# A spectral layer and an MLP on one core: the transforms' steps moved to earlier ticks, and one more block by Strassen's scheme

## Chip, cores and metric

The kernel runs on one core of one Trainium2 chip. The metric is the device time of one execution in microseconds (us). Engines: TensorE (PE; its weight loads are shown as PEld), VectorE (DVE), ScalarE (ACT), GpSimd (POOL) and the queue that issues most DMAs (SP).

## What is computed

```python
# x: (4, 3008, 256); w_r, w_i: (256, 256); w_in: (256, 2048); w_out: (2048, 256)
X = np.fft.rfft(x, axis=1)
Yr = X.real @ w_r - X.imag @ w_i + b_r
Yi = X.real @ w_i + X.imag @ w_r + b_i
Y = shrink(Yr) + 1j * shrink(Yi)          # sign(v) * max(|v| - 0.01, 0)
y = np.fft.irfft(Y, n=3008, axis=1).reshape(12032, 256)
h = y @ w_in
out = (h / (1 + np.exp(-h))) @ w_out
```

All of it is float32; the kernel gets there with pairs of float32r numbers, a high and a low part, so that most products are three matmuls.

## The kernel before

**The MLP** sets the beat. The 12032 tokens are 24 blocks of up to 512, the 2048 hidden units 16 slices of 128. A block and a slice are one *tick*, 384 in all (`ticks`, L1059: slices 0 to 7 of block 0, all of block 1, the rest of block 0 from tick 24 on, then blocks 2 to 23, block i at ticks 16i to 16i+15). In a tick (L1190 to L1228) the recording order is: the shrink left over from the tick before (`deferred`), `split_g` of the tick before (gh on ACT, gl on DVE), `mlp1` (12 matmuls of 256 columns, then Silu on ACT), what the table `fill` has for tick t, `run` (`mlp2` with the slice of two ticks ago: 12 matmuls), and what `fill` has for t + 0.5. Every engine works through its own share of this in order. At a boundary tick, 16i+1, `mlp2` ends block i-1: ACT copies the first half of the accumulators to `o`, DVE the second (L816); in tick 33 DVE also adds the first half of block 0 to both (L819). The same stands at tick 25 for block 1, without the adds.

**Blocks in `FAST`** (10 to 22) do `mlp1` for two slices together by a Strassen scheme (`fast_one`, `fast_more`, `fast_two`, L739 to L785): 7 half products of 3 matmuls in place of 24 matmuls. `fast_moving` (L687, POOL and ACT) makes the sums of x for a block, `fast_weights` (L667) those of w_in, once, after `swap_pools` (L1161) has given up the transforms' pool.

**The transforms** of sequences 1 to 3 lie in the fills (sequence 0 is done before tick 0). Each has 12 units u of two frequencies. `u3_step(b, u, 0)` (L961) issues the DMAs for unit u+2, runs `s2_3(u)` (4 products, PE; casts on ACT and DVE), `split_z(u-2)` (zh on ACT, zl on DVE) and `i1(u-3)` (6 matmuls, then the copy `i1o` on ACT, L505). `u3_step(b, u, 1)` runs `mix3(u-1)` (L447): 6 matmuls into one PSUM bank, which ACT copies to q; then 12 into a second bank, which DVE reads in the shrink (y, L473 to L477). The shrink is deferred to the start of the next tick. Sequences 2 and 3 also need 16 *pieces* each, `stack_split` and `stack_product`. `i2(i)` and `i2_ends(i)` make the columns of block i.

**PSUM** has 8 banks: two of tag h, three acc, and one each of d0, d1 and e0. `bank` (L183) gives d0 and d1 by turns, `third_bank` (L194) gives e0. A matmul that is the first to write a newly given bank waits until the last reader of the bank's use before is done.

**The order of the fills** comes from the loop at L1112: from tick 24 on, each tick gets one stage (a piece, a step or a mix), and none at a boundary tick or one in `taken` (9, 25, and the 16i+1). By its rules the sequences end at ticks 72, 118 and 147.

## Time and profile before

| what | us |
|---|---|
| median of 3 runs (lowest, highest) | 1292.41 (1291.47, 1292.78) |
| the profiled execution: its time, its span | 1294.4, 1291.3 |
| PE busy in the span (10931 matmuls) | 1279.6 |
| DVE, ACT, POOL busy | 894.4, 790.3, 207.1 |

The span runs from the first to the last instruction; 3.1 us of the profiled execution lie around it, and that execution is 2.0 us over the median. Busy times say how much an engine did, not what it held up: who waited for whom is read from the list of waits and the timeline, and what ended last from the chain of waits. A row of the timeline gives start and duration, engine, line and operation; the bracket at its end, the time that the engine stood still before it and who released it. A row of waits gives total us, times and the longest. A row of a stretch gives its length, then busy us (and instructions) of PE, PEld, DVE, ACT and POOL, the granted TensorE clock (1.00 is 2.4 GHz), the DMA engines' share and GB/s.

### The profile page before, as it was taken

The numbers are of one execution on the slowest core, as the hardware profiler recorded it, in microseconds if no ns is written. First come the engines' busy times: TensorE is split into PE (matmuls) and PEld (weight loads), VectorE is DVE, ScalarE is ACT, GpSimd is POOL, SyncE is SP. The second block draws the span as 40 slices with busy tenths as digits, with TensorE's granted clock in tenths as the row PEclk, the third lists the DMA queues.
The fourth block names the chain that finished last, engine by engine and source line by source line (L and its number), as shares of the span: only waits on it lengthen the run. The fifth ranks groups of instructions, "written<-read, shape, count | busy, mean of one in ns | idle before, by whom it ended". The sixth has DMA issues, their size and how long they took to land.

```text
span 1291.3 us, 27533 instructions
## 1 busy us (share of the span) xinstructions
PE 1279.6 (99%) x10931; PEld 1255.5 (97%) x10931; DVE 894.4 (69%) x1703; ACT 790.3 (61%) x1640; POOL 207.1 (16%) x306
## 2 busy tenths in 40 slices
PE   7999999999999999999999999999999999999998
PEld 3989999999999999999999999999999999999998
DVE  4787757878768777666758766667666666676663
ACT  5556655767667657555555666666666666666655
POOL 3001002222212221112202110211012101110200
PEclk8999999999999999999999999999999999999999
DMA  7975514554465543424220111011101110110000
GB/s 263 288 229 191 142 52 122 133 152 109 117 168 148 128 132 99 135 77 122 82 71 2 48 33 29 5 33 33 27 12 34 32 33 1 33 33 14 4 24 25
DMA packets 76296, 110.30 MB, mean 85 GB/s; under 512 B 9008, under 2 KB 54952, under 8 KB 76168
## 3 DMA queue, kind: packets, MB, share of 16 engines
q1 hardware_dynamic: 61921, 79.17, 20.9%
q0 software_dynamic: 10672, 25.68, 7.9%
q10 hardware_dynamic: 3575, 3.70, 0.9%
q8 instruction: 86, 1.41, 0.4%
q14 instruction: 42, 0.34, 0.1%
HBM read 71.03 MB, written 37.49 MB: 84 GB/s over the span
## 4 chain that ended last, share of the span: by engine, by line
PE 97%; DMA 1%; DVE 0%; issue 0%; ACT 0%; POOL 0%; POOLq 0%
PE acc L804 40%; PE h L729 19%; PE h L643 17%; PE mix L454 6%; PE mix L394 3%; PE s L429 2%; PE i L501 2%; PE i2e L570 2%; PE i L570 2%; PE s L281 1%; PE s L320 1%; DMA x_pre<-in_x_dram 1%; PE s L363 1%; PE i L498 1%; PE i L563 1%; PE warm L918 1%
## 5 line engine op out<-in xcount | busy, mean ns | idle before, releaser
L804 PE MATMUL acc<-wout,gh 128*128 128x256 f32 x3008 | 539.8, 277 | 0.3 <-ACT gh L659 0.3
L804 PEld LDWEIGHTS acc<-wout,gh 128*128 128x128 f32 x3008 | 453.8, 188 | 1.5 <-issue 1.0
L804 PE MATMUL acc<-wout,gl 128*128 128x256 f32 x1504 | 415.8, 276 | 0.2 <-DVE gl L660 0.2
L804 PEld LDWEIGHTS acc<-wout,gl 128*128 128x128 f32 x1504 | 282.3, 188 | 0.4 <-DVE gl L660 0.4
L643 PE MATMUL h<-xt,win 128*128 128x256 f32 x2016 | 259.5, 277 | 0.4 <-ACT g L650 0.4
L643 PEld LDWEIGHTS h<-xt,win 128*128 128x128 f32 x2016 | 242.5, 188 | 1.1 <-ACT g L650 0.6
L650 ACT ACTIVATE g<-h 128x512 f32<-128x512 f32 (+1 forms) x177 | 101.9, 576 | 147.9 <-PE h L643 144.4
L780 DVE TENSOR_TENSOR gl<-gp,gh 128x512 fp32r<-128x512 f32 x208 | 145.9, 701 | 25.0 <-ACT gh L779 24.0
L767 ACT ACTIVATE gp<-gp 128x256 f32<-128x256 f32 x104 | 43.4, 417 | 180.1 <-DVE gp L764 180.1
L660 DVE TENSOR_TENSOR gl<-g,gh 128x512 fp32r<-128x512 f32 (+1 forms) x177 | 117.5, 664 | 46.8 <-ACT gh L659 45.1
L779 ACT CAST gh<-gp 128x512 fp32r<-128x512 f32 x208 | 129.3, 622 | 6.6
L659 ACT CAST gh<-g 128x512 fp32r<-128x512 f32 (+1 forms) x177 | 106.1, 600 | 1.1 <-PE acc L804 0.2
L729 PE MATMUL h<-xt,win 128*128 128x256 f32 x624 | 106.2, 279 | 0.0
L769 DVE TENSOR_TENSOR gp<-h,u 128x256 f32<-128x256 f32 x104 | 44.1, 424 | 78.7 <-ACT gp L768 78.7
L473 DVE TENSOR_TENSOR y<-q,mix 64x256 f32<-64x256 f32 x144 | 60.3, 419 | 41.2 <-PE mix L454 30.6
L729 PE MATMUL h<-th,sw_h 128*128 128x256 f32 x312 | 87.4, 280 | 0.0
L729 PEld LDWEIGHTS h<-xt,win 128*128 128x128 f32 x624 | 86.4, 188 | 0.1
L729 PE MATMUL h<-th,sw_l 128*128 128x256 f32 x312 | 86.2, 276 | 0.0
L729 PE MATMUL h<-tl,sw_h 128*128 128x256 f32 x312 | 86.2, 276 | 0.0
L461 POOL TENSOR_TENSOR q<-q,bias 128x256 f32<-128x256 f32 x36 | 29.9, 832 | 335.8 <-ACT q L460 335.8
L764 DVE TENSOR_TENSOR gp<-h,u 128x256 f32<-128x256 f32 x104 | 44.1, 424 | 50.2 <-PE h L729 48.6
L704 POOL TENSOR_TENSOR td<-xf 128x256 f32<-128x256 f32 x13 | 12.3, 948 | 339.0 <-ACT xf L604 260.9
(172 smaller groups left out, 2385.6 us busy)
## 6 DMA issues: line engine op xcount, KB each, us to landing
x_sb<-in_x_dram POOLq DMA_DIRECT2D x70, 188.0 KB, 4.0
a<-scr SPq DMA_DIRECT2D x48, 256.0 KB
gin<-scr SPq DMA_DIRECT2D x48, 192.0 KB
t<-in_c_dram POOLq DMA_DIRECT2D x36, 256.0 KB, 3.6
scr<-i1o SPq DMA_DIRECT2D x36, 256.0 KB
t<-in_c_dram SPq DMA_DIRECT2D x48, 128.0 KB
scr<-s1o SPq DMA_DIRECT2D x32, 192.0 KB
w<-in_moe_w_in_dram SPq DMA_DIRECT2D x8, 512.0 KB
```

What stands on the lines that cost most here:

```text
L454: nc.tensor.matmul(out=out, lhsT=x_[:, e, c, :], rhs=m[:, e, :], start=(n == 0), stop=(n == 5))
L473: nc.vector.tensor_tensor(out=y[64 * i:64 * i + 64, r, :], in0=q[rows, i, :], in1=pv[rows, i, :], op=op,)
L570: nc.tensor.matmul(out=p[:, o:o + NP + RR], lhsT=t[:, q:q + 128], rhs=c4_sb[:, h * (NP + RR):(h + 1) * (NP + RR)], start=(h == 0), stop=(h ...
L643: nc.tensor.matmul(out=p[:, c:c + D], lhsT=w[:, e, f * 128:(f + 1) * 128], rhs=v[:, e, c:c + D], start=(m == 0), stop=(m == 5),)
L650: nc.scalar.activation(out=g[:, q], in_=p[:, q], func=ACTF.Silu)
L659: nc.scalar.copy(gh[:, q], g[:, q])
L660: nc.vector.tensor_sub(gl[:, q], g[:, q], gh[:, q])
L729: nc.tensor.matmul(out=p, lhsT=w[j], rhs=m[k], start=(begins and n == 0), stop=(n == 2), skip_group_check=True,)
L764: nc.vector.tensor_tensor(out=g[:, 1, :], in0=px[:, 0:HB], in1=u, op=ALU.add)
L779: nc.scalar.copy(h, v)
L780: nc.vector.tensor_sub(l, v, h)
L804: nc.tensor.matmul(out=a[:, r, :], lhsT=v[:, q], rhs=wout[:, f, w, :], start=(begins and m == 0 and r == 0), stop=(ends and m == 2), skip_ ...
```

## The change

The loop is rewritten so that more stages fit in a tick. Steps may stand at boundary ticks and at tick 25, and the first is at tick 23 rather than 24. Units 12 to 14 of a sequence, which have no `s2_3`, share a tick with what follows: at ticks 61 and 130 the step of unit 12 and its mix, at tick 107 a step and a piece. In the last sequence the steps of units 5, 7, 9 and 11 take e0 and bring their mix along as a fill at t + 0.5, behind the units of `mlp2` (ticks 120, 123, 126 and 129). The sequences now end at ticks 65, 110 and 132. Before a sequence's first loads all pending stores are issued (`flush(16)`). Block 9 joins `FAST`: `mlp1` loses 192 matmuls of L643 and gains 168 of L729; no other matmul is added or taken away.

```diff
--- before.py
+++ after.py
@@ -34,7 +34,7 @@
 
 STACKED = 2
 
-FAST = range(10, 23)
+FAST = range(9, 23)
 
 X_BUFS = [0, 1, 2, 3, 4, 5, 6, 7, 6, 7, 3, 4, 0, 2, 1, 0]
 BLOCKS = [(c, min(BLK, NT - c)) for c in range(0, NT, BLK)]
@@ -1088,7 +1088,7 @@
         at(0, x_ahead)
         for i in range(2):
             put(5, s1_later, 7, i)
-        for t in (11, 35):
+        for t in (11, 34):
             at(t, x_ahead)
         at(30, nc.gpsimd.dma_start, c5_sb, c5)
         m3 = mix3_weights()
@@ -1108,15 +1108,45 @@
                           for k, fn in enumerate(((i2, i), (i2_ends, i))))
         stacked, last, begun = {1: 18}, 24, set()
         ended = {}
-        done, t, since = 37, 24, 0
+        done, t, since = 34, 23, 0
+        def put_piece(t, since):
+            nonlocal done
+            at(max(t - 2, done), stack_split, *pieces_left[0])
+            at(t, stack_product, *pieces_left[0], since < t - 1)
+            done = t
+            if pieces_left.pop(0)[1] == 15:
+                stacked[max(stacked) + 1] = t
+
+        def put_step(t, since, third=False):
+            nonlocal last
+            b = steps[0][0]
+            if b not in begun:
+                begun.add(b)
+                at(t - 2, flush, 16)
+                for k in range(2):
+                    at(t - 2 + k, u_load, b, k)
+            at(t, u3_step, *steps.pop(0), third or (done == t - 1 and since == t - 2))
+            last = t
+            ended[b] = int(t)
+
+        def can_step(t):
+            if not steps:
+                return False
+            b = steps[0][0]
+            return b in stacked and t >= stacked[b] + (4 if b > 1 else 0)
+
+        def can_put_piece(t, apart):
+            b = steps[0][0] if steps else NB
+            return pieces_left and t >= done + apart and pieces_left[0][0] <= b + 1
+
         while steps or turned:
             boundary = t % NFF == 1 and t > 32
             stage = None
-            if not boundary and t not in taken:
+            if boundary or t == 25 or t not in taken:
                 b = steps[0][0] if steps else NB
-                ready = b in stacked and t >= stacked[b] + (4 if b > 1 else 0)
+                ready = can_step(t)
                 apart = 2 + (ready and b > 1 and len(pieces_left) % 2)
-                if pieces_left and t >= done + apart and pieces_left[0][0] <= b + 1:
+                if not boundary and can_put_piece(t, apart):
                     stage = "piece"
                 elif ready:
                     stage = "mix" if steps[0][2] else "step"
@@ -1126,19 +1156,19 @@
                     more = turned.pop(0)[2]
                     since = t
             if stage == "piece":
-                at(max(t - 2, done), stack_split, *pieces_left[0])
-                at(t, stack_product, *pieces_left[0], since < t - 1)
-                done = t
-                if pieces_left.pop(0)[1] == 15:
-                    stacked[max(stacked) + 1] = t
+                put_piece(t, since)
             elif stage:
-                if b not in begun:
-                    begun.add(b)
-                    for k in range(2):
-                        at(t - 2 + k, u_load, b, k)
-                at(t, u3_step, *steps.pop(0), done == t - 1 and since == t - 2)
-                last = t
-                ended[b] = t
+                b, u, half = steps[0]
+                both = b == NB - 1 and u in (5, 7, 9, 11) and not half and not more
+                put_step(t, since, both)
+                if both:
+                    put_step(t + 0.5, since)
+                    last = since = t
+                if u >= NU and not half and not boundary:
+                    if can_put_piece(t, 2):
+                        put_piece(t, since)
+                    elif can_step(t) and (steps[0][0] > b or steps[0][2]):
+                        put_step(t, since)
             if more:
                 at(t + 0.5 * (stage is not None), *more)
                 if more[0] is i2_ends:
```

Three places in the instruction order, in which every number belongs to one buffer. **VectorE at the end of block 0** (o is the output tile, y the shrunk mix): before, tick 33 has no fill; in the change it has a mix (unit 3 of sequence 1). First before, then the change:

```order
L660 TENSOR_TENSOR gl_2466<-g_2417,gh_2465 128x512
L819 TENSOR_TENSOR o_2495<-o_2495,x_sb1_73 128x512
L816 COPY o_2504<-acc_2114 128x512
L819 TENSOR_TENSOR o_2504<-o_2504,x_sb1_73 128x512
L660 TENSOR_TENSOR gl_2508<-g_2482,gh_2507 128x512
L473 TENSOR_TENSOR y_2568<-q_2527,mix_2537 64x256 x4
```
```order
L660 TENSOR_TENSOR gl_2531<-g_2482,gh_2530 128x512
L819 TENSOR_TENSOR o_2584<-o_2584,x_sb1_73 128x512
L816 COPY o_2593<-acc_2165 128x512
L819 TENSOR_TENSOR o_2593<-o_2593,x_sb1_73 128x512
L473 TENSOR_TENSOR y_2596<-q_2555,mix_2565 64x256 x4
L476 TENSOR_SCALAR q_2555<-y_2596 128x512
L477 TENSOR_TENSOR y_2596<-y_2596,q_2555 128x512
L660 TENSOR_TENSOR gl_2604<-g_2547,gh_2603 128x512
```

The shrink of a mix now comes straight behind the two adds and the copy, where a gl and a whole tick stood between; PE's next instructions that use that bank are the six of `i1` in tick 34.

**ScalarE at a step of the last sequence** (xh and xs from `s2_3`, zh, the copy `i1o`; before, unit 10's at tick 139 and the mix of tick 140; in the change unit 5's at tick 120):

```order
L437 CAST xh_8620<-s2_8615 128x2x256
L438 COPY xs_8622<-s2_8615 128x256
L440 CAST xh_8620<-xs_8622 128x2x128
L486 CAST zh_8629<-y_8587 128x512
L505 COPY i1o_8640<-i1_8633 128x512
L659 CAST gh_8655<-g_8611 128x512
L650 ACTIVATE g_8672<-h_8659 128x512
L460 COPY q_8675<-mix_8674 128x256
```
```order
L437 CAST xh_7665<-s2_7660 128x2x256
L438 COPY xs_7667<-s2_7660 128x256
L440 CAST xh_7665<-xs_7667 128x2x128
L486 CAST zh_7674<-y_7628 128x512
L505 COPY i1o_7685<-i1_7678 128x512
L460 COPY q_7701<-mix_7700 128x256
L659 CAST gh_7731<-g_7652 128x512
```

Between the copy `i1o` and the copy of the next mix (q) there were a gh and a Silu, that is, the Silu of the next tick's `mlp1`; now q follows at once. `i1` and the second product of that mix have the same bank (d0 at ticks 120 and 126, d1 at 123 and 129).

**ScalarE at the end of the last sequence** (before: ticks 143 and 144; in the change ticks 129 and 130):

```order
L650 ACTIVATE g_8857<-h_8844 128x512
L486 CAST zh_8859<-y_8833 128x512
L505 COPY i1o_8870<-i1_8863 128x512
L659 CAST gh_8885<-g_8857 128x512
L650 ACTIVATE g_8902<-h_8889 128x512
L460 COPY q_8905<-mix_8904 128x256
```
```order
L486 CAST zh_8335<-y_8293 128x512
L505 COPY i1o_8346<-i1_8339 128x512
L816 COPY o_8355<-acc_7275 128x512
L460 COPY q_8366<-mix_8365 128x256
L659 CAST gh_8396<-g_8317 128x512
L650 ACTIVATE g_8413<-h_8400 128x512
L486 CAST zh_8415<-y_8389 128x512
L505 COPY i1o_8426<-i1_8419 128x512
L460 COPY q_8429<-mix_8428 128x256
```

The last mix's q follows directly on the `i1o` of the same tick, whose zh needs the y of the mix that stands at tick 129.5. At tick 130, as at tick 61, `i1` and the mix's second product both have d0.

## Rows read from the trace of the kernel before

**Rows 1.** Page, part 4: the chain that ended last, by engine.
```profile
PE 97%; DMA 1%; DVE 0%; issue 0%; ACT 0%; POOL 0%; POOLq 0%
```
**Rows 2.** The longest of PE's waits; the stretch from 125 to 1290.
```profile
PE s L281 <- DMA x_pre<-in_x_dram: 4.6, 1, 4.6
...
125.00:1290.00 1165.00, 1162.27 (x10201) 1161.85 (x10199) 807.36 (x1552) 719.88 (x1505) 194.13 (x280) 1.00 0.25 68
```
**Rows 3.** Timeline of PE in block 8 (start us, us, engine, line, operation).
```profile
594.16 0.39 PE L804 MATMUL acc<-wout,gh 128*128 128x256 f32 x2
...
595.52 1.52 PE L643 MATMUL h<-xt,win 128*128 128x256 f32 x12
596.88 1.05 PE L429 MATMUL s<-t,a 128*128 128x128 f32 x8
597.69 0.36 PE L501 MATMUL i<-zh,t 128*128 128x256 f32 x1
...
598.48 0.40 PE L804 MATMUL acc<-wout,gh 128*128 128x256 f32 x2
```
**Rows 4.** Timeline of ACT, the same ticks.
```profile
599.63 0.62 ACT L486 CAST zh<-y 128x512 fp32r<-128x512 f32 x1
600.16 0.58 ACT L505 COPY i1o<-i 128x512 f32<-128x512 f32 x1
```
**Rows 5.** Timeline of DVE, the same ticks.
```profile
594.43 1.72 DVE L473 TENSOR_TENSOR y<-q,mix 64x256 f32<-64x256 f32 x4 [2.18 <-PE mix L454]
...
596.64 0.69 DVE L477 TENSOR_TENSOR y<-y,q 128x512 f32<-128x512 f32 x1
```
**Rows 6.** Timeline of PE and DVE at ticks 25 and 26.
```profile
173.47 0.39 PE L804 MATMUL acc<-wout,gh 128*128 128x256 f32 x2
...
176.19 1.13 PE L570 MATMUL i<-c_sb,gin 120*128 120x141 f32 x8
177.06 0.37 PE L804 MATMUL acc<-wout,gh 128*128 128x256 f32 x1
...
175.03 0.69 DVE L816 COPY o<-acc 128x512 f32<-128x512 f32 x1 [1.14 <-PE acc L804]
175.64 0.68 DVE L660 TENSOR_TENSOR gl<-g,gh 128x512 fp32r<-128x512 f32 x1
```
**Rows 7.** Timeline of PE and DVE at tick 33, the end of block 0.
```profile
204.92 0.39 PE L804 MATMUL acc<-wout,gh 128*128 128x256 f32 x2
...
206.42 0.69 DVE L819 TENSOR_TENSOR o<-o,x_sb 128x512 f32<-128x512 f32 x1 [0.78 <-DMA scr<-i1o]
...
207.78 0.70 DVE L819 TENSOR_TENSOR o<-o,x_sb 128x512 f32<-128x512 f32 x1
208.39 0.68 DVE L660 TENSOR_TENSOR gl<-g,gh 128x512 fp32r<-128x512 f32 x1
```
**Rows 8.** Timeline of ACT and PE at tick 1: a wait for a bank.
```profile
101.84 0.58 ACT L650 ACTIVATE g<-h 128x512 f32<-128x512 f32 x1
...
102.47 1.68 PE L643 MATMUL h<-xt,win 128*128 128x256 f32 x12 [0.36 <-ACT g L650]
```
**Rows 9.** Timeline of PE and ACT at tick 67, a step without `s2_3`.
```profile
339.28 0.28 PE L501 MATMUL i<-zh,t 128*128 128x256 f32 x1
...
340.50 0.59 ACT L505 COPY i1o<-i 128x512 f32<-128x512 f32 x1
```
**Rows 10.** PE and DVE at a piece, tick 68; page, part 6: a 256 KB load.
```profile
342.68 0.62 PE L320 MATMUL s<-sx,c_sb 128*128 128x256 f32 x4
...
344.12 1.28 DVE L325 TENSOR_TENSOR s1o<-s,s1o 48x512 f32<-48x512 f32 x2 [1.78 <-ACT s1o L324]
...
t<-in_c_dram POOLq DMA_DIRECT2D x36, 256.0 KB, 3.6
```
**Rows 11.** Two stretches near the start.
```profile
22.00:25.00 3.00, 0.05 (x1) 0.08 (x1) 0.00 (x0) 0.00 (x0) 0.00 (x0) 0.50 0.96 303
25.00:29.00 4.00, 4.00 (x5) 1.56 (x6) 0.00 (x0) 0.89 (x2) 0.00 (x0) 0.53 0.53 190
```

## The prediction

> **What bounds the kernel now.** I read the chain of waits first: 97% of it is PE [rows 1], so only what PE executes, or waits for, counts. Then PE's own list of waits: its longest wait, 4.6 us, is for the first data of x, and from 125 us to 1290 us not one wait is listed; PE is busy for 1162.27 of those 1165.00 us [rows 2]. What is short of that sum is records missing from the trace, for the timeline shows matmul behind matmul. So in the whole stretch that the change touches there is nothing to win by shortening a wait. There are only matmuls to leave out, and waits to make. The pitch of a matmul of 256 columns is read off two starts: 12 of `mlp1` from 595.52 to 596.88, that is 1.36 us or 0.1133 each [rows 3].
>
> **What is removed.** Block 9 by the Strassen scheme: 16 ticks of 12 matmuls become 8 pairs of 21, so 192 - 168 = 24 matmuls go. 24 x 0.1133 = **2.72 us** less on PE, and nothing else of PE's work changes in number. What block 9 adds elsewhere (POOL's sums, VectorE's five small adds a pair, ScalarE's copies) runs beside PE, as it does for blocks 10 to 22 in the same order and distance, where PE waits for none of it [rows 2]. The sums of block 9 end at tick 140 and are needed at 144, one tick nearer than block 10's; a tick without fills is 24 matmuls, 2.72 us, so if that cover went, what is lost would be counted in tenths. Cost taken: nothing.
>
> **What is moved, and what it makes PE wait for.** The steps themselves cost PE the same at any tick. What changes is how soon PE comes back to a PSUM bank whose last reader is still at work. A matmul starts 0.05 us after such a reader ends: Silu ends at 101.84 + 0.58 = 102.42, `mlp1` starts at 102.47 [rows 8]. Counting the banks that `bank` and `third_bank` hand out, I find nine places where PE comes back sooner than the readers allow by the rows.
>
> *Tick 26.* Tick 25 is a boundary and now has a mix. The copy of the accumulators stands before the shrink on VectorE, and waits for the last units: it starts 175.03 - 173.47 = 1.56 us after `mlp2` began, and the next instruction starts at 175.64, 2.17 after [rows 6]. The four y instructions then take 1.72 [rows 5]: the bank is free 2.17 + 1.72 + 0.05 = 3.94 after the mix ends. PE needs it for the second half of `i2`, after `mlp2` 1.36, `mlp1` 1.36 and half of the 177.06 - 176.19 = 0.87 of `i2` [rows 6], at 3.15. **Wait 0.79.**
>
> *Tick 34.* At tick 33 two adds stand there too: from the start of `mlp2`, 204.92, the next instruction of VectorE starts only at 208.39, 3.47 later [rows 7]. Free at 3.47 + 1.72 + 0.05 = 5.24. PE needs it for `i1` after 1.36 + 1.36 + 0.81 (`s2_3`, 596.88 to 597.69 [rows 3]) = 3.53. **Wait 1.71.**
>
> *Tick 61.* Step and mix of unit 12 in one tick. `i1` starts at 339.28 and its copy ends at 340.50 + 0.59 = 341.09 [rows 9], 1.81 later, with 0.05 1.86. Now PE wants that bank for the mix's second product after `i1` (6 matmuls, 0.68) and the first product (6, 0.68), at 1.36. **Wait 0.50.**
>
> *Ticks 120, 123, 126, 129.* The copy of `i1` ends at 600.16 + 0.58 = 600.74 [rows 4], and the bank is free at 600.79. PE, after `i1`, does `mlp2` from 598.48 [rows 3], 1.36, and the mix's first product, 0.68: it is at the bank at 600.52. **Wait 0.27, four times: 1.08.** Taking e0 for `s2_3` doesn't help here, since it is not that bank that is late.
>
> *Tick 130.* The mix at 129.5 is the last thing PE does in its tick, so its shrink starts with tick 130. From a mix's end (594.16 [rows 3]) to the end of y takes 596.64 + 0.69 - 594.16 = 3.17 [rows 5]. Only then can ScalarE make zh, and the copy of `i1` stands behind zh: 0.05 + 0.53 (zh to copy) + 0.58 [rows 4] + 0.05 = 4.38. PE is there after `mlp1`, `i1` and the first product, 1.36 + 0.68 + 0.68 = 2.72. **Wait 1.66.**
>
> *Two near misses, at nothing.* At tick 115 VectorE's copy in boundary tick 113 pushes the reading of `s2_3` late; by the same rows it ends 0.2 before PE comes, and if it doesn't, 0.4 is lost. At tick 70 the first data of sequence 2 are asked for at tick 68, behind the store of a piece made in the same tick (the new `flush(16)` puts it in front on SP's queue). That piece's data are ready 344.12 + 1.28 - 342.68 = 2.72 after its product starts [rows 10], and PE comes 0.45 (four matmuls) + 1.36 + 2.72 + 1.36 = 5.89 after it. That leaves 3.2 us for a store's and two loads' issue and 256 KB; POOL's queue takes 3.6 for as much [rows 10], so the cost lies between 0 and about 1.5. I take 0, since the two other sequences' first loads have the same four ticks.
>
> **The sum.** -2.72 + 0.79 + 1.71 + 0.50 + 1.08 + 1.66 = **+3.02 us**. The profiled execution took 1294.4, so one like it would take 1297.4; the median of the runs is 1292.41, and the forecast for it is **1295.4 us** (+0.23%). About 0.2%, 2.6 us, is what a measurement of this kernel can tell from no change, so the forecast lies just beyond it. Reading each wait 0.1 us shorter or longer, and the near misses at their upper ends in part, the case spans 1294.6 to 1296.3.
>
> The rows show PE without a wait while its banks d0 and d1 change turns with a tick's work between two uses [rows 2]. The Trainium skill, page "Perfetto Trace Analysis", section "Matmuls", says that independent groups should rotate through different banks so that the evacuation of one overlaps the next group's matmuls. The trace of before agrees, by having no wait; by that rule alone, with rotation still at work in the change, the sum would be -2.72, and where the change gives the next group the bank just left, it speaks against it.
>
> **Rivals.** *The banks come free in time, and it is faster.* Place: the same nine. If ScalarE's copy and VectorE's y are done before PE is there, all that is left is block 9: 1292.41 - 2.72 = 1289.7. It decides at 0.27 us in the four doubled ticks, 0.50 at 61, 0.79 at 26 and 1.7 at 34 and 130. For it speaks that the old order, which also took steps in every tick from 119 on, never waits. Against it, that the order of instructions on VectorE and ScalarE is fixed, and the rows of each chain leave little to shorten. Chance 0.08, of which 0.06 is faster by over 0.2%.
>
> *Half the waits.* Each chain is taken from a tick with its own work in front; in the change's ticks ScalarE or VectorE may have less in front, above all at 34 and 130, where the waits are long. With 2.5 to 4.7 us of waits in place of 5.74 the time is 1292.2 to 1294.4: no change. Chance 0.20.
>
> *The clock falls in a long wait.* At the start PE stood for 4.6 us, and the granted clock was 0.50 in the stretch from 22 to 25 us, 1.2 GHz, and 0.53 in the next four, in which PE was busy throughout [rows 11]. That wait is the only long one in the trace, so a wait of 1.7 us at tick 34 or 130 lies between none and it, nearer to none. If the clock does fall, some 7 us of matmuls (22 to 29 us) run at half the rate, and 3.4 us are lost: 1298.8. Chance 0.10, all of it slower. The Trainium skill, page "TensorE: Matmul & The Clock Gate", section "HAM oscillation", tells of kernels whose clock falls in each wait for data; the start of this trace agrees, no later stretch shows it.
>
> *The load at tick 70 is late* by 1 to 1.5 us: about 1296.7. Chance 0.07.
>
> *That the change doesn't do what it says* is excluded by the order of the instructions, which has the 168 matmuls in place of 192 and the last step at tick 132.
>
> **How the numbers follow.** My case has a chance of 0.55. The limit of 0.2% lies at 1295.0 and cuts it, about three quarters above: 0.42 slower, 0.13 no change. With the rivals: slower 0.42 + 0.10 + 0.06 = 0.58; within 0.2%, 0.13 + 0.20 + 0.02 + 0.01 = 0.36; faster 0.06. The range goes from 1292.4, which leaves out the full gain, to 1298.8, one fall of the clock; the case's own is 1294.6 to 1296.3.
>
> **What would show it.** In the list of PE's waits after 125 us there should be: `mix` released by ACT's `i1o` copy (L505) six times, 3.2 us together, the longest 1.7; `i1` released by VectorE's y (L473), once, 1.7; `i2` released by the same, once, 0.8. No wait of PE in ticks 144 to 160, and L643 with 1824 matmuls, L729 with 2352. The granted clock stays at 1.00 from 125 us on. The prediction is wrong if the list stays empty (then 1289.7), if waits stand at other places, such as `s2_3` for a load, or if the clock shows 0.5 anywhere after 125 us.

## The result and the profile after

The changed kernel took **1306.62 us** (median of 6 runs, 1302.94 to 1309.87) against 1292.35 of the kernel before beside it (6 runs, 1291.47 to 1292.84): ratio 1.011, 95% interval 1.0099 to 1.0121. It is 14.3 us slower; forecast were 3.0. The profiled execution is the longest of the six, 1309.87, with a span of 1308.1. Of all executions of changed kernels below one was slow, 1837.59 us, among the eleven with three weight parts moved, and its kernel's median is that of the other ten.

The page, parts 1 (busy us, share, instructions) and 4 (the chain), to set beside [rows 1]:

```profile
PE 1284.7 (98%) x10907; PEld 1257.2 (96%) x10907; DVE 910.5 (70%) x1743; ACT 796.2 (61%) x1662; POOL 213.8 (16%) x314
...
PE 92%; DMA 3%; DVE 1%; ACT 1%; issue 1%; SPq 1%; POOL 0%; DVEq 0%; ACTq 0%; POOLq 0%
```

10907 matmuls are 24 fewer than before, as counted, and yet PE is busy longer, 1284.7 in place of 1279.6: some of them ran at a lower clock. And the chain has DMA, DVE and SP's queue in it, where PE alone held 97% [rows 1]. The list of PE's waits, which had one long wait at the start and none after 125 us [rows 2], now reads:

```profile
PE s L429 <- DMA a<-scr: 5.1, 1, 5.1
...
PE acc L804 <- ACT gh L659: 2.2, 1, 2.2
PE mix L454 <- ACT i1o L505: 1.6, 2, 1.3
PE i L501 <- issue: 1.6, 1, 1.6
...
PE acc L804 <- DVE gl L660: 1.3, 2, 1.1
PE i L570 <- DVE y L473: 0.8, 1, 0.8
```

Three of these are forecast: `mix` behind i1o, `i` (L501, tick 34, here put down to "issue") and `i2` (L570, tick 26) behind y. The row of 2.2 lies before 125 us, in ticks the change does not touch, and belongs to this execution (below); behind it, from 111 to 114 us, the granted clock was 0.50. The two others were priced at nothing: **`s2_3` of sequence 2 waits 5.1 us for its first data at tick 70**, and `mlp2` waits 1.1 for gl at tick 140.

The forecast waits in PE's timeline, at ticks 26, 34, 61 and 130 (the bracket is the wait; those of ticks 120 to 129, 0.2 each, are too short for one):

```profile
183.92 0.72 PE L570 MATMUL i<-c_sb,gin 120*128 120x141 f32 x4 [0.78 <-DVE y L473]
...
220.36 0.36 PE L501 MATMUL i<-zh,t 128*128 128x256 f32 x1 [1.60 <-issue]
...
330.52 0.50 PE L454 MATMUL mix<-wi,xh 128*128 128x256 f32 x2 [0.33 <-ACT i1o L505]
...
635.28 0.51 PE L454 MATMUL mix<-wi,xh 128*128 128x256 f32 x2 [1.29 <-ACT i1o L505]
```

Around tick 70, SP's timeline, then the chain of waits (start, us, what), then stretches of the span, the first of them near the early wait (PEclk is the third number from the end):

```profile
346.73 8.51 SPq L208 DMA_DIRECT2D out_dram<-o  x11
355.34 3.47 SPq L208 DMA_DIRECT2D scr<-s1o  x2
...
362.43 0.38 SPq L354 DMA_DIRECT2D a<-scr  x1
```

```profile
355.34 7.03 DMA scr<-s1o
...
362.43 4.41 DMA a<-scr
```

```profile
111.00:114.00 3.00, 3.00 (x16) 3.00 (x16) 2.90 (x6) 1.68 (x4) 0.00 (x0) 0.50 0.57 217
...
219.00:223.00 4.00, 2.64 (x23) 2.67 (x24) 3.87 (x8) 0.99 (x4) 3.07 (x5) 1.00 0.58 127
...
367.00:370.40 3.40, 3.40 (x16) 3.40 (x17) 0.46 (x2) 0.86 (x2) 0.00 (x0) 0.50 0.50 172
...
633.00:638.00 5.00, 3.71 (x31) 3.49 (x30) 3.29 (x7) 2.03 (x5) 1.48 (x2) 1.00 0.34 111
```

SP issues eleven stores of block 3's output (boundary tick 65 ended that block), then the store of sequence 2's last piece at 355.34, and only at 362.43 the load that tick 70 needs: the load reads what that store writes, and the store, behind the outputs, took 7.03 us to land. In the kernel before, the outputs of that boundary had long gone when the load came, seven ticks behind it; here it comes three ticks behind. When PE goes on at 366.97, the granted clock is 0.50, 1.2 GHz, and in 367.0 to 370.4 PE does 16 matmuls, though it never stops: 1.7 us more. Behind the waits at ticks 34 and 130 the clock stayed at 1.00.

At ticks 137 to 140, PE, DVE and POOL:

```profile
668.85 0.39 PE L804 MATMUL acc<-wout,gl 128*128 128x256 f32 x1 [1.09 <-DVE gl L660]
...
659.38 1.23 DVE L660 TENSOR_TENSOR gl<-g,gh 128x512 fp32r<-128x512 f32 x1
...
663.35 1.25 DVE L660 TENSOR_TENSOR gl<-g,gh 128x512 fp32r<-128x512 f32 x1
...
668.11 0.68 DVE L660 TENSOR_TENSOR gl<-g,gh 128x512 fp32r<-128x512 f32 x1
...
657.76 1.15 POOL L704 TENSOR_TENSOR td<-xf 128x256 f32<-128x256 f32 x1 [20.62 <-ACT xf L604]
...
664.00 1.20 POOL L713 TENSOR_TENSOR td<-xf,td 128x256 f32<-128x256 f32 x1
```

In these rows VectorE's gl, while POOL makes block 9's sums, takes 1.23 to 1.25 us, and 0.68 when POOL is through. From 658 to 670 VectorE has no gap, since the weights' sums for the Strassen scheme stand in the same ticks, and the last gl comes too late. My theory after this profile: the nine waits were rightly forecast, and two more losses, tick 70 (6.9 us with the clock) and block 9's start (1.3 or more), make up the rest.

### The profile page after: what moved, and what is told of

It is laid out like the page before. It is cut to its first block, busy times and chain, and to the rows that moved or that the text cites. A ratio compares the mean times of both kernels' runs of the same rounds, so it can differ in the third digit from the quotient of the medians.

```text
span 1308.1 us, 27564 instructions
## 1 busy us (share of the span) xinstructions
PE 1284.7 (98%) x10907; PEld 1257.2 (96%) x10907; DVE 910.5 (70%) x1743; ACT 796.2 (61%) x1662; POOL 213.8 (16%) x314
## 4 chain that ended last, share of the span: by engine, by line
PE 92%; DMA 3%; DVE 1%; ACT 1%; issue 1%; SPq 1%; POOL 0%; DVEq 0%; ACTq 0%; POOLq 0%
PE acc L804 38%; PE h L729 20%; PE h L643 14%; PE mix L454 5%; PE s L429 3%; PE mix L394 3%; PE i L501 2%; PE i2e L570 2%; PE i L570 2%; PE s L320 1%; DMA x_pre<-in_x_dram 1%; DMA scr<-s1o 1%; PE s L363 1%; PE s L281 1%; PE i L498 1%
## 5 line engine op out<-in xcount | busy, mean ns | idle before, releaser
L643 PE MATMUL h<-xt,win 128*128 128x256 f32 x1824 | 236.0, 278 | 0.3 <-ACT g L650 0.3
L643 PEld LDWEIGHTS h<-xt,win 128*128 128x128 f32 x1824 | 220.7, 189 | 1.1 <-issue 0.5
L780 DVE TENSOR_TENSOR gl<-gp,gh 128x512 fp32r<-128x512 f32 x224 | 157.2, 702 | 26.7 <-ACT gh L779 26.0
L650 ACT ACTIVATE g<-h 128x512 f32<-128x512 f32 (+2 forms) x161 | 92.4, 574 | 128.8 <-PE h L643 127.9
L779 ACT CAST gh<-gp 128x512 fp32r<-128x512 f32 x224 | 139.2, 621 | 7.1
L660 DVE TENSOR_TENSOR gl<-g,gh 128x512 fp32r<-128x512 f32 (+2 forms) x161 | 107.1, 666 | 47.1 <-ACT gh L659 45.6
L729 PE MATMUL h<-xt,win 128*128 128x256 f32 x672 | 114.4, 279 | 0.0
L769 DVE TENSOR_TENSOR gp<-h,u 128x256 f32<-128x256 f32 x112 | 47.6, 425 | 84.7 <-ACT gp L768 84.7
L659 ACT CAST gh<-g 128x512 fp32r<-128x512 f32 (+2 forms) x161 | 96.2, 598 | 1.1 <-PE acc L804 0.2
L729 PE MATMUL h<-th,sw_h 128*128 128x256 f32 x336 | 94.2, 280 | 0.0
L729 PEld LDWEIGHTS h<-xt,win 128*128 128x128 f32 x672 | 93.0, 188 | 0.5 <-DVE gp L764 0.2
L729 PE MATMUL h<-th,sw_l 128*128 128x256 f32 x336 | 92.9, 276 | 0.0
L729 PE MATMUL h<-tl,sw_h 128*128 128x256 f32 x336 | 92.8, 276 | 0.0
L764 DVE TENSOR_TENSOR gp<-h,u 128x256 f32<-128x256 f32 x112 | 47.6, 425 | 55.3 <-PE h L729 53.9
```

Source lines behind the costliest of these rows:

```text
L643: nc.tensor.matmul(out=p[:, c:c + D], lhsT=w[:, e, f * 128:(f + 1) * 128], rhs=v[:, e, c:c + D], start=(m == 0), stop=(m == 5),)
L650: nc.scalar.activation(out=g[:, q], in_=p[:, q], func=ACTF.Silu)
L659: nc.scalar.copy(gh[:, q], g[:, q])
L660: nc.vector.tensor_sub(gl[:, q], g[:, q], gh[:, q])
L729: nc.tensor.matmul(out=p, lhsT=w[j], rhs=m[k], start=(begins and n == 0), stop=(n == 2), skip_group_check=True,)
L764: nc.vector.tensor_tensor(out=g[:, 1, :], in0=px[:, 0:HB], in1=u, op=ALU.add)
```

## Experiments

Each run is set beside the changed kernel's 1306.62, and each group of runs had the kernel before on the same chip (1292.6 to 1293.4), so that between groups some 0.8 us say nothing. Line numbers of edited kernels are a few higher.

### The changed kernel again

No edit.

> The changed kernel once more, unaltered. Theory (two waits that I did not price, at ticks 70 and 140, are part of the order and recur; the 3.3 us that the first profile lost in ticks 2 to 5 are that execution's own): 1303 to 1308 us, the wait of TensorE for sequence 2's first data at tick 70 again 5 to 5.5 us with the granted clock at 0.5 for some 3.4 us after it, the wait for gl at tick 140 again 1.1 to 1.3 us, and the wait in ticks 2 to 5 back at 0.3 us as before the change. Rival (the early loss belongs to the change, since pools lie elsewhere from the start): 2.2 us of wait and 3.4 us of half clock before 125 us again.

Measured: 1306.62 us (1303.28 to 1307.26), ratio 1.0103 (1.0088 to 1.0118). Waits of 4.6 at tick 70, 1.1 at tick 140, 0.8, 1.6 and 1.3 at the forecast places. The wait before 125 us was 0.6 where it had been 2.2 (1.5 at most in the other traces): the early loss was the first execution's own, and the rest belongs to the order.

### Tick 70: what holds the load

First the load was issued earlier, in two steps. The store of sequence 2's last piece was put in front of the outputs:

```diff
+        if (b, q) == (2, 15):
+            stores.insert(0, (v[:, h, g * 4 * D:(g + 1) * 4 * D], o))
+        else:
+            store(v[:, h, g * 4 * D:(g + 1) * 4 * D], o)
```

> One piece's store, that of sequence 2's last, goes to the front of the list of stores, ahead of the outputs of block 3. Theory (the load of sequence 2's first data waits for this store, whose packets come behind eleven output stores): the load issues at about 358.7 us in place of 362.4, as soon as the store of the piece of tick 68 ahead of it on SP has gone; the wait at tick 70 falls from 5.3 to about 1.5 us and the granted clock holds after it, since it held after the waits of 1.8 and 1.5 us at ticks 34 and 130: 5.5 us less than the changed kernel. Rival A (the 256 KB transfer itself is slow beside other traffic): the wait stays at 5 us, no gain. Rival B (only the store of tick 68's own piece, that the new flush puts ahead of the load, holds it): no gain either, load at 362.4.

In the second run the load of tick 68 stands ahead of that tick's piece as well:

```diff
-                at(t - 2, flush, 16)
-                for k in range(2):
-                    at(t - 2 + k, u_load, b, k)
+                fill.setdefault(t - 2, [])[:0] = [(flush, (16,)), (u_load, (b, 0))]
+                at(t - 1, u_load, b, 1)
```

> As the run with that store in front, and the flush and the load of tick 68 also go ahead of that tick's piece, so that its store no longer stands before the load on SP. Theory: the load issues by about 355 us, lands before TensorE is there, no wait and no fall of the clock at tick 70: 6.9 us less than the changed kernel (wait 5.2, clock 1.7), of which 1.4 is what the run with the store alone leaves. Rival A (slow transfer): no better than the changed kernel. Rival B (the piece of tick 68 alone is at fault): the same 6.9 us, but the run with the store alone gains nothing.

Measured: 1308.35 (1308.01 to 1308.77) and 1306.28 (1305.72 to 1307.13): no gain. **My theory fell.** The load was issued at 356.83 and 356.04 us, near what I had said (358.7 and 355), but it did not land in time. The chain of waits of the first of the two runs, and two stretches:

```profile
356.83 7.87 DMA a<-scr
```

```profile
361.00:363.00 2.00, 0.00 (x0) 0.00 (x0) 0.00 (x0) 0.00 (x0) 0.00 (x0) 0.50 1.16 244
...
367.00:369.00 2.00, 2.00 (x11) 2.00 (x11) 1.20 (x3) 1.51 (x4) 0.00 (x0) 0.50 0.01 4
```

and of the second:

```profile
356.04 6.89 DMA a<-scr
```

The load took 7.87 and 6.89 us in place of 4.41. How much earlier it was issued can't be read off 356.83, 356.04 and 362.43, since what a trace loses near its start shifts all that follows. It is counted from the moment PE arrives at the step, the start in these rows (the changed kernel, the first run, the second) less the wait in the bracket, 361.87, 357.96 and 357.58:

```profile
366.97 2.04 PE L429 MATMUL s<-t,a 128*128 128x128 f32 x8 [5.10 <-DMA a<-scr]
...
364.83 2.05 PE L432 MATMUL s<-t,a 128*128 128x128 f32 x8 [6.87 <-DMA a<-scr]
...
363.07 2.05 PE L432 MATMUL s<-t,a 128*128 128x128 f32 x8 [5.49 <-DMA a<-scr]
```

The load goes out 0.6 us behind that moment in the changed kernel and 1.1 and 1.5 ahead of it in the two runs: 1.7 and 2.1 us earlier, no more. For SP, with the piece's store in front, first stands until that piece is made, and the eleven outputs follow later, here in the first run, 10.8 us ahead of PE in place of 15.1 (346.73):

```profile
347.18 8.72 SPq L208 DMA_DIRECT2D out_dram<-o  x11
```

The trace also has sixteen landings for each such load. In the second run fourteen of them come within 2.8 us of the issue, one at 3.8 and the last at 6.9; in the first, fifteen within 4.9 and the last at 7.9. So most of the load passes, and PE waits for the last sixteenth. The DMA engines' share is 0.97 and 0.91 from 357 to 365 us. In the first run the clock fell while PE still waited and stayed at 0.50 until 370.9, so that run is even slower than the changed kernel. The wait for the store ahead of it was only one thing in the load's way.

So the outputs themselves were held back until the first two loads are out, with the load ahead of the piece as above, and the piece's store in its old place:

```diff
-                store(pairs[n, p0:p0 + m, :], o[k:k + m, :])
+                (held.append if i == 3 else stores.append)((pairs[n, p0:p0 + m, :], o[k:k + m, :]))
...
+                if b == STACKED:
+                    at(t - 1, give_back)
```

> The eleven output stores of block 3 (512 rows of 1 KB) are held back until both first loads of sequence 2 are out (given back at tick 69), and the load of tick 68 goes ahead of that tick's piece; all else as changed. The two runs that moved the load itself forward (issue at 356.8 and 356.0 in place of 362.4) gained nothing, so the theory now: DMA queues of SP work in the order of issue, and the 256 KB of the load come only behind the outputs' 1 KB packets, that last until about 361 us. Then the load, alone behind the store of sequence 2's last piece, lands before TensorE asks for it: wait at tick 70 under 0.5 us (from 4.6 to 5.5), granted clock 1.00 throughout, 5 to 7 us less than the changed kernel. Rival (the loads of x on POOL's queue, at the same time, are what slow it): the wait stays above 2.5 us.

Measured: **1298.62 us** (1297.35 to 1299.51), ratio 1.0046 (1.0032 to 1.0060): 8.0 less. SP's timeline, PE's first matmul of the step, and the stretch around it:

```profile
346.20 0.30 SPq L213 DMA_DIRECT2D scr<-s1o  x1
...
348.94 0.38 SPq L359 DMA_DIRECT2D a<-scr  x1
...
355.49 1.58 SPq L213 DMA_DIRECT2D out_dram<-o  x4
...
357.20 1.05 PE L434 MATMUL s<-t,a 128*128 128x128 f32 x8
```

```profile
340.00:375.00 35.00, 35.00 (x309) 35.00 (x309) 22.48 (x33) 24.59 (x44) 7.66 (x14) 1.00 0.68 184
```

The load goes out at 348.94, before the first output at 355.49, and PE is busy for all of 35 us at clock 1.00. The loads of x on POOL's queue run here as they did there, so the rival that blamed them falls. What held the load was the outputs ahead of it on SP: with them behind, fifteen of its landings come within 3.4 us and the last at 4.0. Whether they held it by their order in the queue or by the share that they took of the DMA engines no run separates, nor was the holding tried without the load ahead of the piece. The Trainium skill, page "DMA: Bandwidth & Descriptors", section "Queues, rings and completion order", says that each DMA engine consumes the descriptors of a queue's ring in order; the one late landing of a load that was issued behind eleven stores, at 7.87 us, agrees but does not prove it.

### The nine bank waits

First try: the third bank, e0, for the mix's second product at ticks 25 and 33 and for `i1` at the six others. As it ran, the rule went by tick, so at ticks 61 and 130, where step and mix share a tick, both took e0:

```diff
-        p = bank("mix")
+        p = third_bank("mix") if apart else bank("mix")
...
-        p = bank("i1")
+        p = third_bank("i1") if apart else bank("i1")
...
+THIRD = (25, 33, 61, 120, 123, 126, 129, 130)
```

> At ticks 25 and 33 the mix's second product takes the third PSUM bank, e0, and at ticks 61, 120, 123, 126, 129 and 130 the inverse product i1 takes it (the doubled ticks' s2_3 goes back to d0 and d1); all else as in the changed kernel. Theory (nine waits for a PSUM bank whose reader is late, 5.5 us in sum): all nine fall below 0.1 us and the time is 5.5 us less than the changed kernel's. Rival (the readers are late for other reasons, and the wait moves to the next user of e0 or to the next reader in the queue): less than half of that, and new waits of 0.3 us or more within two ticks of those nine.

Measured: 1304.24 (1300.43 to 1305.13), 2.4 less. The waits at ticks 26, 120, 123, 126 and 129 are gone. At 61 and 130 they stayed, as both products had one bank again (0.33 and 1.6). And for the wait of tick 34 came another, one tick later:

```profile
219.51 0.47 PE L456 MATMUL mix<-wr,xh 128*128 128x256 f32 x2 [1.13 <-DVE xl L443]
```

Here the rival holds: a bank does not help where VectorE is late, with two adds and a copy in front of the shrink; what it makes next, xl, is as late. So in the second try `i1` alone takes e0 at the six ticks, and at ticks 25 and 33 the shrink is written right behind the mix:

```diff
             fills(t)
+            if t in (25, 33):
+                while deferred:
+                    deferred.pop(0)()
...
+THIRD = (61, 120, 123, 126, 129, 130)
```

> The nine bank waits once more. In the first try ticks 61 and 130 gave e0 to i1 and to the mix's second product alike, and the wait stayed; here e0 goes to i1 alone at 61, 120, 123, 126, 129 and 130, and at ticks 25 and 33 the shrink of the mix is written right behind the mix, ahead of the boundary's copy and adds on VectorE, with no bank moved. Theory (the wait of tick 34 is the order on VectorE: with a bank moved it came again as a wait for xl one tick later): all nine waits under 0.2 us, also none for xl at tick 35, and 5 to 5.5 us less than the changed kernel (1301 to 1302). Rival (VectorE's work in the boundary ticks is too much in any order): 0.8 us or more of wait stays at ticks 34 to 36, 4 us less at most.

Measured: **1299.35 us** (1297.31 to 1300.72), 7.3 less. All that is left of PE's waits from 125 us to 1290 us:

```profile
PE s L431 <- DMA a<-scr: 4.6, 1, 4.6
PE acc L806 <- DVE gl L662: 1.1, 1, 1.1
```

All nine are gone, the one at tick 34 by the order on VectorE alone. By the starts of the same matmuls in this trace and the changed kernel's second one, the nine places took 6.35 us: 5.5 of waits, and some 0.1 at each because PE picks up slowly; what the medians show beyond that is within their ranges. At tick 130 the first two matmuls behind the wait start at 635.28, the third at 635.63, 0.35 later, where the pair after it takes 0.22 (635.75 to 635.97).

### Block 9

Block 9 back in the plain form, all else as changed:

```diff
-FAST = range(9, 23)
+FAST = range(10, 23)
```

> The change without its first line: blocks 10 to 22 by Strassen's scheme, block 9 in the plain form, all else as changed. Theory (block 9 saves 24 matmuls, 2.7 us, and gives back 1.2 us in a wait for gl at tick 140 and some 0.5 us at ticks 146 to 148): 1.0 us more than the changed kernel, and no wait for gl at tick 140. Rival (it gives back nothing that the order would not lose anyway): 2.7 us more. Second rival (POOL's sums of block 9 cost more than they win): the same time or less than the changed kernel.

Measured: 1306.86 (1305.05 to 1309.39), no difference by the medians. The wait for gl at tick 140 is gone. The trace of this run had only 3.0 us of wait at tick 70, so I take the way behind it: from the first matmul of the piece at tick 71 to the same Strassen matmul of block 10 it needs 728.43 - 366.30 = 362.13 us, the changed kernel's second trace 730.75 - 369.51 = 361.24. So 0.9 is what block 9 wins net of its 2.72.

POOL's sums one a tick in place of two:

```diff
-                    at(t + 1 + (k if first == 16 * i - 13 else k // 2), next, moving, None)
+                    at(t + 1 + k, next, moving, None)
```

> The eight parts of block 9's sums on POOL and their copies are given out one a tick, ticks 137 to 144, in place of two a tick, 137 to 140; nothing else. Theory (POOL's instructions slow VectorE's beside them, 0.69 to 1.23 us, and two a tick make gl late): VectorE's gl instructions of ticks 138 to 140 fall back towards 0.7 us, the wait at tick 140 to under 0.2 us, 1.1 to 1.8 us less than the changed kernel. Rival (gl is late because of fast_weights, four to five VectorE instructions a tick, whatever POOL does): the wait stays at 1 us or more.

Measured: 1305.06 (1303.95 to 1306.53), 1.6 less by the medians, with intervals that overlap. But the trace shows no such gain: the wait for gl is gone, and the first Strassen pair of block 9 waits for another instruction of VectorE in its place (gp is the tile in which VectorE adds up the half products of a pair):

```profile
PE h L729 <- DVE gp L756: 0.9, 1, 0.9
```

The weights' sums, one part every second tick:

```diff
-            at(last + 2 + q * 3 // 2 + k, next, steps, None)
+            at(last + 2 + q * 2 + k, next, steps, None)
```

> The sums of the weights, fast_weights, are begun every second tick for one part each in place of three parts in two ticks beginnings; POOL's sums as in the changed kernel. Theory (POOL's share is what makes gl late): the wait at tick 140 is only partly cut, to 0.4 to 1.0 us, since POOL still slows VectorE; the time 0.3 to 0.8 us less. Rival (VectorE's load by fast_weights alone): wait under 0.2 us, 1.2 us less.

Measured: 1309.52 (1308.54 to 1312.04), 2.9 **more**: waits for gp of 1.8 (three, the longest 1.4) and 0.9 in the first pairs, and 1.2 for gl. Neither theory nor rival had that. What these runs say together is that VectorE has no room: take its work out of one tick, and PE waits in the one it goes to.

### All of it together

The edits shown above in one kernel: the piece's store and the load ahead, the first try of the banks, and POOL's sums one a tick.

> The store and load of sequence 2 in front, the third bank at the nine places, and block 9's sums one a tick, together. Theory (these are the whole of the loss and add up): 6.9 + 5.5 + 1.2 to 1.8 less than the changed kernel, so 1290 to 1293 us, at or up to 0.2% below the kernel before; in the trace no wait of TensorE over 0.3 us between 125 us and the end. Rival (waits uncovered behind those taken away): 1295 or more with new waits.

Measured: 1304.36 (1303.34 to 1304.96), the rival's number, since two of its parts did not work: 5.6 us at tick 70, and the waits at 35, 61 and 130. Then the second versions, outputs held, `i1` alone on e0 and the shrink ahead, with the sums one a tick, and this kernel once more beside the last runs:

> Outputs of block 3 held and the load ahead, i1 on e0, the shrink ahead at the boundaries, block 9's sums one a tick: all together. Theory (the waits found are the whole loss, and add): 6 to 7 + 5 to 5.5 + 1.5 less than the changed kernel's 1306.6, so 1292.5 to 1294, within 0.2% of the kernel before; what the 24 matmuls of block 9 win is eaten by about 1 us that the first Strassen pairs wait for VectorE and some 0.6 in other places. Rival A (no other loss): 1290. Rival B (the load's wait is not cured): 1299 or more.

> The run with all once more beside these, for its spread: 1291.5 to 1293, wait for gp at tick 144 again 0.9 us, no other over 0.4 us after 125 us.

Measured: **1292.25 us** (11 runs, 1290.96 to 1296.74), ratio 1.0001 (0.9989 to 1.0013); once more beside the last runs 1292.11 (1290.89 to 1293.98), ratio 0.9991 (0.9983 to 1.0000). The parts add up: 8.0 + 7.3 = 15.3 by the single runs, 14.4 here (14.1 without the third edit, below). One wait is left from 125 us on:

```profile
PE h L736 <- DVE gp L763: 0.9, 1, 0.9
```

The same edits with block 9 in the plain form (`FAST = range(10, 23)`, so no sums of its own):

> As the run with all, but with block 9 in the plain form. Theory (block 9 in the Strassen form wins 2.7 us and costs about 1): 1.5 to 2 us more than the run with all. Rival (VectorE, filled without a gap from tick 134 to 147 by the sums of the weights, gives the whole 2.7 back): no difference, or faster than the run with all.

Measured: 1293.64 (11 runs, 1292.37 to 1296.94), with no wait of PE listed after 125 us. By the medians block 9 wins 1.4 us, with ranges that overlap. The traces say 1.0: from the Silu of tick 132, first with block 9 in the Strassen form and then without, to the end of the span it is 1289.8 - 624.82 = 664.98 us and 1291.7 - 625.72 = 665.98.

```profile
624.82 0.60 ACT L657 ACTIVATE g<-h 128x512 f32<-128x512 f32 x1 [0.25 <-PE h L650]
...
625.72 0.60 ACT L657 ACTIVATE g<-h 128x512 f32<-128x512 f32 x1 [0.25 <-PE h L650]
```

So with nothing else in the way block 9 wins 1.0 to 1.4 us of its 2.72, less than the theory's 1.5 to 2.

Whether the rest can be had was asked with two of eight weight parts made at ticks 147 and 150, when the Strassen ticks have begun:

```diff
-            at(last + 2 + q * 3 // 2 + k, next, steps, None)
+            at(last + 2 + (0, 1, 3, 4, 6, 7, 13, 16)[q] + k, next, steps, None)
```

> As the run with all, but the last two of the eight weight parts (needed at ticks 156 and 158) are made from ticks 147 and 150 on in place of 143 and 144. Theory (VectorE is full from tick 134 to 147, two parts are 4.4 us of its work): the wait of the first Strassen pair for gp, 0.9 us, goes to under 0.2, no new wait over 0.3 us; 0.8 to 1.2 us less than the run with all. Rival (the parts are in the way wherever they stand, as in the run that spread them all): new waits for gp of 0.5 us or more at ticks 147 to 153, no gain.

then with POOL's sums two a tick again (`k // 2` as in the change) and the weights as changed:

> As the run with all, but POOL's sums of block 9 two a tick again, as in the changed kernel. Theory (VectorE is full, and POOL only shifts where the lag shows): the wait for gl at tick 140 is back with 1.1 us, the one for gp at tick 144 goes; within 0.5 us of the run with all. Rival (the spreading itself is worth what it won in the changed kernel, 1.5 us): 1 us or more slower than the run with all.

and with sums two a tick and three parts late:

```diff
-            at(last + 2 + q * 3 // 2 + k, next, steps, None)
+            at(last + 2 + (0, 1, 3, 4, 6, 9, 13, 16)[q] + k, next, steps, None)
```

> Sums two a tick as changed, and the last three weight parts from ticks 143, 147 and 150 on. Theory (room on VectorE is all that is missing, but the lag at tick 140 comes before the parts that are moved): wait for gl at tick 140 still 1.1 us, none for gp; 0.2 to 0.8 us more than the run with two parts later and spread sums. Rival (POOL alone): the same time as the run with sums together, whatever the weights do.

Measured: 1294.49 (1292.82 to 1296.03), 1292.51 (1291.64 to 1295.74) and 1295.40 (1294.12 to 1297.59), beside 1292.11 of the run with all on the same chip. The waits of the first (with a stretch behind them) and of the second:

```profile
PE h L736 <- DVE gp L763: 1.6, 1, 1.6
PE h L736 <- DVE gp L771: 1.0, 1, 1.0
```

```profile
684.00:688.00 4.00, 4.00 (x23) 3.82 (x23) 2.94 (x6) 1.37 (x4) 0.00 (x0) 0.66 0.02 4
```

```profile
PE acc L811 <- DVE gl L667: 1.1, 1, 1.1
```

The third has waits of 1.6 and 1.1 for gp, where its theory said none, and 1.1 for gl. Moving weight parts later costs 2.4 us (the first beside the run with all) and 2.9 (the third beside the second), the first rival's case: they stand in front of gp. Behind the first run's two waits the clock was 0.66 for four us, which the third, with the same two waits, does not show. Spreading POOL's sums or not is worth 0.4 us, less than the runs' spread, and only changes which instruction is late. Every wait that these orders move about is ended by VectorE, so its time between tick 134 and the first pairs is what limits block 9; how much of that time is POOL's doing no run separates, and an order that hides it all was not found.

## Why the prediction was right or wrong

**Removed matmuls: right.** L643 has 1824 and L729 2352, 24 fewer in sum, 2.72 us.

**The nine waits: right in place and size.** Found at tick 26 0.94 (forecast 0.79), at 34 1.76 (1.71), at 61 0.50 (0.50), at the four doubled ticks 0.84 together (1.08) and at 130 1.45 (1.66), each as the distance of the starts less one pitch of 0.113: 5.5 against 5.74. Two small things were missed: the slow start behind each, 0.1, and that tick 34's wait is one of VectorE's order, which a third bank does not cure. The rivals "the banks free in time" and "half the waits" fell.

**"Two near misses, at nothing": here it failed.** Tick 115 shows no wait, as priced. At tick 70 the working counted what stands in front of the load in its own tick, the piece's store, and gave 3.2 us for it and 256 KB; it took 0 of a range up to 1.5, "since the two other sequences' first loads have the same four ticks". The store that the load waits for is another, that of sequence 2's last piece, which took 7.03 us to land behind block 3's outputs. The sequences have the same ticks, but not the same queue: sequence 3's first load comes twelve ticks behind a boundary, sequence 2's now three, with those eleven outputs still going out. I looked at what SP issues, and not at what its queue still has to move. Measured: 5.1 and 4.6 us of wait; with the clock's part 6.9 and 6.4 us from the Silu of tick 66 to that of tick 72, beside the run that held the outputs back, and 8.0 by that run's median. A wait of `s2_3` for a load and a clock of 0.5 were among the prediction's own signs of being wrong.

**The clock.** The rival put a fall of the clock behind the bank waits of 1.7 us, at 3.4 us, from the start of the kernel before [rows 11]; it took all of 22 to 29 us for matmuls at half the rate, though PE stood for the first three of the seven. The bank waits did not bring it about (1.00 in 219 to 223 and 633 to 638). The wait at tick 70 did, and it cost 1.7: 3.4 us at half the rate. The late load and the clock stood as two rivals, 0.07 and 0.10, each alone; they are one chain, and together they lie outside the range. The Trainium skill, page "TensorE: Matmul & The Clock Gate", section "HAM oscillation", describes just this, a wait for data and then a cold start; the trace agrees at tick 70, and shows no cold start behind the waits of 1.6 and 1.3 us.

**"Block 9 ... Cost taken: nothing": failed.** The argument was that PE waits for none of this in the same order and distance. The order is right, and the one tick less was named; what was not read is how little room VectorE had. Two rows of the kernel before, of the ticks before block 10, 5 to 6 ticks ahead of its first pair (a stretch; VectorE's timeline):

```profile
689.00:693.00 4.00, 4.00 (x38) 4.00 (x37) 3.93 (x7) 3.19 (x7) 3.44 (x5) 1.00 0.01 2
...
692.10 1.24 DVE L660 TENSOR_TENSOR gl<-g,gh 128x512 fp32r<-128x512 f32 x1
```

There too the weights' sums, gl and POOL's sums meet, VectorE is busy for 3.93 of 4 us, gl takes 1.24 us, and PE goes on without a wait, just so. For block 9 the first pair is one tick nearer, and the last part of x that VectorE splits ahead of the sums is 464 columns and 0.64 us (657.66) where block 10's is 78 and 0.24 (683.04). Which of the two used up the margin no run separates; together they cost 1.8 us in the changed kernel (2.72 less the 0.9 that is won) and 1.3 to 1.7 with the rest cured, at tick 140 or in the first pairs, where the prediction spoke of tenths. The prediction looked at the waits of PE, which were none, and not at the busy share behind them. The Trainium skill, page "SBUF — State Buffer", section "SBUF: two separate sides", says that VectorE and GpSimd share a pair of ports under a lock, which an instruction of VectorE with two inputs from SBUF needs when GpSimd reads there. gl at 1.23 beside POOL and 0.68 without agrees, and so does the rest of the changed kernel's profile: the 40 gl that start ahead of a POOL instruction beside them take 0.68 to 0.69 us, and the 15 that start while one runs take some 0.55 us more than what it still has to run (0.69 us with 0.15 left, 1.28 with 0.73).

**The sum** from the kernel before to the second trace of the changed one: -2.7 + 6.35 (nine waits) + 6.4 (tick 70) + 1.4 (tick 140) + 0.3 (first pairs) = 11.8 of 14.0 by the medians. Three steps at ticks 81, 91 and 97 start `i1` 0.23 late each, 0.7; what is left, 1.5, lies in the first 150 us and in the scatter, and no run settles it. That the result is slower was forecast; three quarters of it, 10.4 of 14.0, have another reason.

## What to carry to other kernels

When a step is moved, look at what its queue still has to move at that moment, not only at what is issued in front of it: a load behind 512 KB of stores was as late when it was issued 2 us earlier, and holding the stores back by a few ticks cost nothing. A stretch without waits can still have no margin: read the busy share of the helping engines there before more is put in front of them. And two rivals that cause one another have to be priced together.

## What the hardware showed that was not expected

- The granted clock fell to 0.50 with the waits of 3.0 to 6.9 us at tick 70 and behind one of 2.2 us before 125 us, and never behind one alone of 1.1 to 1.6 us; after two of 1.0 and 1.6 us some 11 us apart it was 0.66 for four us in one run, and held in another.
- A 256 KB load took 4.4 us when issued late and 7.9 us when issued 1.7 us earlier behind the same stores; of its sixteen landings fifteen had come at 4.9.
- PE takes about 0.1 us more for the first two matmuls behind a wait for a bank (0.35 us in place of 0.22 at tick 130).
- VectorE's gl, a difference of two SBUF operands of 128x512, takes 0.68 us alone or when it starts ahead of POOL's instruction, and up to 1.28 us when POOL's is running as it starts.
